# Weight stream operations per inner block of the first feed-forward stage: nine in both halves, or nine and then twelve

## The chip, the cores and the metric

The kernel runs on one core of a Trainium2 chip. The time that counts is the device time of one execution, in microseconds (us). Every number below comes from the times of the kernel before or from one profiled execution of it. TensorE is called PE here, VectorE DVE, ScalarE ACT, GpSimd POOL and SyncE SP.

## The reference

Three stages follow one another: a pooled attention, a feed-forward stage with ELU (here MoE 1), and a feed-forward stage with RMS norm and SwiGLU (MoE 2).

```python
q_pool = q.reshape(B, H, S // 2, 2, D).mean(axis=3)
attn = softmax(q_pool @ k.T / sqrt(D));  x = attn @ v         # x: 1152 tokens x 512
h = x @ w_in                                                  # MoE 1: 512 -> 2048
g = where(h > 0, h, exp(min(h, 0)) - 1);  x = g @ w_out       # 2048 -> 512
xn = x / sqrt(mean(x * x) + 1e-6) * rms_g                     # MoE 2
out = (silu(xn @ w_gate) * (xn @ w_val)) @ w_out2             # 512 -> 1536 -> 512
```

The weights of MoE 1 and MoE 2 arrive as 64-bit floating point numbers; activations are float32.

## The kernel before, in words

Every product is made of three: each operand is split into a high part and a low part, and `product` (lines 162 to 169) adds high x high (L167), low x high (L168) and high x low (L169) for four slices of the inner dimension, so one product of a 128 x 128 x 4 weight tile with a chunk of 384 tokens is twelve matmuls. The 1152 tokens are three chunks, c = 0, 1, 2.

MoE 1 runs in two halves, `hf` = 0 and 1. A half first has eight *inner blocks* (i = 0 to 7): block i multiplies one weight tile with the three chunks, each into a PSUM bank of its own (eight banks go round), and hands each result to `elu`. I write (i, c) for such a unit. `elu` runs, for a unit: on ACT two activations (L183, L184) into a tile e; then it flushes what the unit before left pending, the rounding of its e to the high part `gh` (ACT, L188) and the low part `gl` = e - gh (POOL, L63; for c = 1 of the second half DVE, L69); then steps of the weight stream; then on DVE L187, which reads e and the PSUM bank and so frees the bank; then two more steps of the stream. After the eight blocks comes the *out phase* of the half: products of `gh` and `gl` with the tiles of w_out; for each output tile m first those of blocks 0 to 3 (q = 0) for the three chunks, then those of blocks 4 to 7 (q = 1), slice by slice.

In the second half's out phase the results are added to x (DVE, L607) and squared for the norm (ACT L561; sums on POOL, the last on DVE, L563). The last two output tiles go chunk by chunk, and between them stand the two small PE jobs of the norm of the chunk before: `sums` (six matmuls, L568, which need the DVE's L563), and one product later `scale` (three transposes, L578, which need DVE's reciprocal L572, which needs ACT's root L571). DVE's L581 then scales x.

The *weight stream* turns a 64-bit weight tile into a high and a low float32 part. It is a generator over 68 tiles, nine steps for a tile: ACT L113, DVE L115, (two steps on the tile before, once its buffer is chosen: ACT L141 makes its high part `wh`, POOL L63 its low part `wl`), DVE L120, L122, L124 (after which SP starts a later tile's DMA, L90) and L128. `ws.step(i, k)` runs k steps, and stops early where the stream has got eight tiles ahead of tile i. Nothing is scheduled at run time: each engine runs its instructions in the order in which the program emitted them, so the numbers of steps at the calls set the order on DVE, ACT, POOL and SP.

Of the kernel before, what the change touches and what calls it, by code (L numbers as in the profile page):

```python
# [38 lines left out]
def tile_kernel(ctx: ExitStack, tc: tile.TileContext, qd, kd, vd, w1d, w2d, wgd, wvd, wod, rgd, outd):  # L39
# [120 lines left out]
    cs = lambda c: slice(c * CH, (c + 1) * CH)  # L160

    def product(out, w, a, first, last, ks=range(4)):

        wh, wl = w
        for k in ks:
            ah, al = a(k)
            PE.matmul(out, lhsT=wh[:, k, :], rhs=ah, start=first and k == 0, stop=False)  # L167
            PE.matmul(out, lhsT=wh[:, k, :], rhs=al, start=False, stop=False)  # L168
            PE.matmul(out, lhsT=wl[:, k, :], rhs=ah, start=False, stop=last and k == 3)  # L169

    def xchunk(c):
        return lambda k: (xh[:, k, cs(c)], xl[:, k, cs(c)])
# [3 lines left out]
    def flush():  # L176
        while pending:
            pending.pop(0)()

    def elu(ps, gh, gl, lo):  # L180

        e = hp.tile([128, CH], F32, tag="e", name="e", bufs=4)
        T.activation(out=e, in_=ps, func=AF.Relu, scale=-1.0)  # L183
        T.activation(out=e, in_=e, func=AF.Exp, scale=-1.0)  # L184
        flush()
        ws.step(wi, 1)
        V.scalar_tensor_tensor(out=e, in0=e, scalar=-1.0, in1=ps, op0=ALU.add, op1=ALU.max)  # L187
        pending.append(lambda: (T.copy(gh, e), lo(gl, e, gh)))  # L188
        ws.step(wi, 2)
# [178 lines left out]
    def emit_x(p, xs, a=0, b=QS):  # L368
# [7 lines left out]
        else:  # L376
# [5 lines left out]
    wi = 0  # L382
    ge = tuple(gep.tile([128, NE, CH], F32R, name=f"ge{n}", tag=f"ge{n}") for n in "hl")
    ws = Stream(w_in[:NE] + [w for hf in range(2) for w in
                             (w_in[8:16] if hf else w_in[NE:8]) + [w_out[4 * (2 * hf + q) + m] for m in range(4) for q in range(2)]]
                + [w[i] for i in range(12) for w in (wgd, wvd)] + [wod[i] for i in range(12)])
# [20 lines left out]
    for n in range(ns):  # L407
        p, k = n // NPT, n % NPT
# [112 lines left out]
    for n in range(NE):  # L521
        elu(fb[:, n, 0:CH], ge[0][:, n, :], ge[1][:, n, :], lo_pool)
# [12 lines left out]
    def bank():  # L535

        nonlocal nbank
        n, nbank = nbank % 8, nbank + 1
        if n == 5 and len(psb) == 1:
            with tc.using_default_side("right"):  # L540
                psb.append(ctx.enter_context(tc.tile_pool(name="psC", bufs=3, space=PSUM)))
        return psb[n >= 5].tile([128, 512], F32, tag="b", name="b", bufs=3 if n >= 5 else 5)[:, 0:CH]

    gh, gl = (gp.tile([128, 8, NT], F32R, name=f"g{n}", tag=f"g{n}") for n in "hl")

    def g_quad(hf, q, c):
        return lambda k: ((ge[0][:, k], ge[1][:, k]) if hf == c == q == 0 and k < NE else
                          (gh[:, 4 * q + k, cs(c)], gl[:, 4 * q + k, cs(c)]))
# [40 lines left out]
    wi = 0  # L589
    for hf in range(2):  # L590
        for i in range(8):
            w = ws.get(wi)
            for c in range(3):
                if hf == 0 and c == 0 and i < NE:
                    continue
                ps = bank()
                product(ps, w, xchunk(c), True, True)
                elu(ps, gh[:, i, cs(c)], gl[:, i, cs(c)], lo_dve if c == 1 and hf else lo_pool)
            wi += 1
        flush()  # L600

        def out1(c, m, q, b, w):
            product(b, w, g_quad(hf, q, c), q == 0, q == 1)
            if q == 1:
                x = x2[:, m, cs(c)]
                if hf:
                    V.tensor_tensor(out=x, in0=b, in1=x, op=ALU.add)  # L607
                    norms[c].square(m)
                else:
                    T.copy(x, b)  # L610

        for m in range(2 if hf else 4):
            bs = [bank() for c in range(3)]
            for q in range(2):
                for c in range(3):
                    out1(c, m, q, bs[c], ws.get(wi + q))
                    ws.step(wi + q, 4)
            wi += 2
        if hf:
            T.activation(out=dummy, in_=eps, func=AF.Sqrt)  # L620
            for c in range(3):
                for n in range(4):
                    m, q = 2 + n // 2, n % 2
                    if q == 0:
                        b = bank()
                    out1(c, m, q, b, ws.get(wi + n))
                    if c < 2 or n < 2:
                        ws.step(wi + (n if c == 2 else 0), 3)
                    if c and n == 1:
                        norms[c - 1].sums()  # L630
                    if c and n == 2:
                        norms[c - 1].scale()
            wi += 4
# [103 lines left out]
```

## Time and profile before

| | |
|---|---|
| median of three runs | 696.57 us (695.61 to 697.49) |
| the profiled execution | 696.5 us, span 694.7 us |
| PE busy | 680.0 us (98%) |
| DVE busy | 538.2 us (77%) |
| ACT busy | 415.0 us (60%) |
| POOL busy | 372.6 us (54%) |

The profile's times count from the span's start. The second half of MoE 1 has its inner blocks on PE from 355.8 to 405.5 us, and its out phase from there to about 463 us. A timeline row gives the start, the duration, the engine, the line, the operation, output and inputs, and in brackets how long the engine had been idle and on whom it waited. PE's matmuls overlap: a row of 0.34 us starts 0.17 us after the one before, and the spacing is the cost.

### The profile page before, as it was taken

The page shows a single profiled execution, that of the slowest core. Times are in us where ns is not written, and L with a number is a line of the kernel's source. Part 1 is how long each engine was busy: PE and PEld are TensorE (multiplying, and loading weights), DVE is VectorE, ACT ScalarE, POOL GpSimd, SP SyncE. Part 2 cuts the span into 40 slices and gives each one's busy share as a digit, 9 for nine tenths or more (in the row PEclk, how much of TensorE's full clock was granted, in tenths as well). Part 3 has the DMA queues.
Part 4 walks back from the last instruction along what each step waited for, and adds up shares of the span by engine and source line. Part 5 has one row for each costly group of instructions (what it writes and reads, how often), then busy time and mean ns, then how long its engine had stood idle before and what let it go on. Part 6 is the DMA issues. An engine that isn't in the chain of part 4 may idle for free.

```text
span 694.7 us, 11366 instructions
## 1 busy us (share of the span) xinstructions
PE 680.0 (98%) x4243; PEld 668.1 (96%) x4243; DVE 538.2 (77%) x891; ACT 415.0 (60%) x855; POOL 372.6 (54%) x332
## 2 busy tenths in 40 slices
PE   7999999999999999999999999799999999999998
PEld 6999999989898999999999999799999999999997
DVE  6888889898999877999959999866999876584000
ACT  5888889789888857774447764334444443342000
POOL 5988788897978405674434544532554343342000
PEclk9999999999999999999999999999999999999999
DMA  5423323432432000213422123201323222232000
GB/s 181 144 86 113 128 87 103 144 119 87 134 129 72 1 31 32 92 60 129 145 92 85 67 86 127 91 1 38 116 92 121 92 97 92 87 106 80 35 35 34
DMA packets 21607, 62.34 MB, mean 90 GB/s; under 512 B 2736, under 2 KB 4784, under 8 KB 21552
## 3 DMA queue, kind: packets, MB, share of 16 engines
q1 hardware_dynamic: 21552, 61.62, 26.2%
q8 instruction: 33, 0.54, 0.3%
q14 instruction: 22, 0.18, 0.1%
HBM read 59.25 MB, written 2.36 MB: 89 GB/s over the span
## 4 chain that ended last, share of the span: by engine, by line
PE 78%; DVE 15%; ACT 4%; issue 1%; DVEq 0%; ACTq 0%
PE b L167 16%; PE b L169 16%; PE b L168 16%; PE s L279 10%; PE o L323 9%; PE t L297 8%; DVE p L283 3%; DVE ptl L69 2%; DVE wt L124 2%; DVE wt L128 2%; DVE wt L120 1%; DVE gl L69 1%; DVE e L187 1%; DVE wt L122 1%; ACT gh L188 1%
## 5 line engine op out<-in xcount | busy, mean ns | idle before, releaser
L167 PE MATMUL b<-xh,wh 128*128 128x384 f32 x468 | 157.3, 336 | 0.6 <-ACT sl L638 0.6
L169 PE MATMUL b<-xh,wl 128*128 128x384 f32 x468 | 157.1, 336 | 0.0
L168 PE MATMUL b<-xl,wh 128*128 128x384 f32 x468 | 157.0, 335 | 0.0
L63 POOL TENSOR_TENSOR wl<-wt,wh 128x512 fp32r<-128x512 f32 x68 | 98.4, 1447 | 76.6 <-ACT wh L141 48.2
L283 DVE TENSOR_SCALAR_CACHE_REDUCE p<-s 128x1152 f32<-128x1152 f32 x72 | 97.4, 1354 | 21.1 <-PE s L279 20.7
L69 DVE TENSOR_TENSOR ptl<-t,pth 128x384 fp32r<-128x384 f32 x216 | 106.7, 549 | 3.5 <-ACT pth L305 3.0
L279 PE MATMUL s<-kd,qt 128*128 128x384 f32 x480 | 98.0, 341 | 5.6 <-DVE p L283 4.6
L305 ACT CAST pth<-t 128x384 fp32r<-128x384 f32 x216 | 89.3, 486 | 23.1 <-PE t L297 22.5
L288 ACT ACTIVATE p<-p,st 128x1152 f32<-128x1152 f32 x72 | 91.4, 1269 | 5.2 <-DVE p L283 4.9
L279 PEld LDWEIGHTS s<-kd,qt 128*128 128x128 f32 x480 | 81.5, 188 | 9.0 <-DVE p L283 4.0
L167 PEld LDWEIGHTS b<-xh,wh 128*128 128x128 f32 x468 | 87.9, 188 | 0.9 <-ACT sl L638 0.9
L168 PEld LDWEIGHTS b<-xl,wh 128*128 128x128 f32 x468 | 87.9, 188 | 0.0
L169 PEld LDWEIGHTS b<-xh,wl 128*128 128x128 f32 x468 | 87.9, 188 | 0.0
L297 PE MATMUL t<-ident,p 128*128 128x128 f32 x648 | 85.9, 275 | 0.0
L323 PE MATMUL o<-pth,vd 128*128 128x256 f32 (+1 forms) x288 | 84.4, 315 | 0.0
L297 PEld LDWEIGHTS t<-ident,p 128*128 128x128 f32 x648 | 73.9, 141 | 6.8 <-DVE ptl L69 4.3
L323 PE MATMUL o<-ptl,vd 128*128 128x256 f32 (+1 forms) x288 | 78.4, 295 | 0.0
L113 ACT ACTIVATE wt<-wr 128x512 f32<-128x512 f32 x68 | 45.7, 672 | 51.2 <-POOL wl L63 31.8
L124 DVE SCALAR_TENSOR_TENSOR wt<-wr,wt 128x512 uint32<-128x512 uint32 x68 | 73.2, 1076 | 1.4
L128 DVE CUSTOM_DVE_ANT_0 wt<-wt,we 128x1024 uint16<-128x1024 uint16 x68 | 66.7, 981 | 1.9
L63 POOL TENSOR_TENSOR gl<-e,gh 128x384 fp32r<-128x384 f32 x37 | 40.2, 1087 | 44.5 <-ACT gh L188 42.8
L167 PE MATMUL b<-gh,wh 128*128 128x384 f32 x180 | 61.5, 342 | 0.0
(113 smaller groups left out, 1321.3 us busy)
## 6 DMA issues: line engine op xcount, KB each, us to landing
wr<-in_w_dram SPq DMA_DIRECT2D x32, 512.0 KB, 3.2
rawk<-in_k_dram SPq DMA_DIRECT2D x32, 288.0 KB, 2.9
rawq<-in_q_dram SPq DMA_DIRECT2D x15, 576.0 KB, 3.9
wr<-in_wg_dram SPq DMA_DIRECT2D x12, 512.0 KB, 3.2
wr<-in_wv_dram SPq DMA_DIRECT2D x12, 512.0 KB, 3.2
wr<-in_wo_dram SPq DMA_DIRECT2D x12, 512.0 KB, 3.2
rawv<-in_v_dram SPq DMA_DIRECT2D x16, 288.0 KB, 2.8
out_dram<-o SPq DMA_DIRECT2D x12, 192.0 KB, 1.8
```

What stands on the lines that cost most here:

```text
L63: G.tensor_tensor(out=o, in0=i, in1=f(h), op=ALU.subtract)
L69: V.tensor_tensor(out=o, in0=i, in1=f(h), op=ALU.subtract)
L124: V.scalar_tensor_tensor(out=t, in0=hi, scalar=0x80000000, in1=t, op0=ALU.bitwise_and, op1=ALU.bitwise_xor)
L167: PE.matmul(out, lhsT=wh[:, k, :], rhs=ah, start=first and k == 0, stop=False)
L168: PE.matmul(out, lhsT=wh[:, k, :], rhs=al, start=False, stop=False)
L169: PE.matmul(out, lhsT=wl[:, k, :], rhs=ah, start=False, stop=last and k == 3)
L279: PE.matmul(s[:, m, 0:384], lhsT=a, rhs=b[:, 384 * m:384 * m + 384], start=n == 0, stop=n == len(parts) - 1)
L283: V.tensor_scalar(out=pt, in0=s[:, :, 0:384], scalar1=-0.0625, scalar2=None, op0=ALU.mult, op1=ALU.min, accum_out=st[p][:, 0, TILES[i][4], :])
L288: T.activation(out=pt, in_=pt, func=AF.Exp, scale=-1.0, bias=st[p][:, 0, TILES[i][4], :], accum_out=st[p][:, 1, TILES[i][4], :])
L297: PE.transpose(ps[:, k, :], src[:, 128 * b:128 * b + 128], ident)
L305: T.copy(oh, re(ps))
L323: PE.matmul(self.o[:, 0:self.N], lhsT=v[:, b, :], rhs=(pth, ptl)[u][:, g["buf"], b, g["c0"]:320], start=self.n == 0, stop=self.n == 17)
```

## The change

`elu` takes the number of steps that it runs before L187 as an argument, 1 if nothing is said. The inner blocks of MoE 1 pass 1 in the first half and 2 in the second. With the two steps behind L187 that makes 3 x 3 = 9 steps in a block of the first half and 3 x 4 = 12 in one of the second. The calls for the three units at the end of the attention are as they were.

```diff
-    def elu(ps, gh, gl, lo):
+    def elu(ps, gh, gl, lo, k=1):
...
-        ws.step(wi, 1)
+        ws.step(wi, k)
...
-                elu(ps, gh[:, i, cs(c)], gl[:, i, cs(c)], lo_dve if c == 1 and hf else lo_pool)
+                elu(ps, gh[:, i, cs(c)], gl[:, i, cs(c)], lo_dve if c == 1 and hf else lo_pool, 1 + hf)
```

PE's and SP's instructions stand in the same order in both kernels. On DVE in the second half's inner blocks, from L187 of unit (0, 2), one block before has these nine rows:

```order
L187 SCALAR_TENSOR_TENSOR e<-e,b 128x384
L124 SCALAR_TENSOR_TENSOR wt<-wr,wt 128x512
L128 ISA wt<-wt,we 128x1024
L187 SCALAR_TENSOR_TENSOR e<-e,b 128x384
L115 TENSOR_SCALAR we<-wr 128x512
L187 SCALAR_TENSOR_TENSOR e<-e,b 128x384
L120 TENSOR_SCALAR wt<-wt 128x512
L69 TENSOR_TENSOR gl<-e,gh 128x384
L122 TENSOR_SCALAR wt<-wt 128x512
```

With the change the rows from the same L187 on are (wr, wt and we are the stream's tiles, b the PSUM bank):

```order
L187 SCALAR_TENSOR_TENSOR e<-e,b 128x384
L115 TENSOR_SCALAR we<-wr 128x512
L187 SCALAR_TENSOR_TENSOR e<-e,b 128x384
L120 TENSOR_SCALAR wt<-wt 128x512
L122 TENSOR_SCALAR wt<-wt 128x512
L124 SCALAR_TENSOR_TENSOR wt<-wr,wt 128x512
L128 ISA wt<-wt,we 128x1024
L187 SCALAR_TENSOR_TENSOR e<-e,b 128x384
L115 TENSOR_SCALAR we<-wr 128x512
L69 TENSOR_TENSOR gl<-e,gh 128x384
L187 SCALAR_TENSOR_TENSOR e<-e,b 128x384
L120 TENSOR_SCALAR wt<-wt 128x512
```

Three blocks now hold four tiles' worth of stream rows, and the pattern repeats every three blocks (32 rows) instead of every block (nine). From the first L187 of the half to the last, 13 stream rows more stand on DVE. They are missing later: between that last L187 and the first L572 of the norm DVE has 13 rows fewer. The end of that stretch, on DVE (sq and x are the norm's sums and the stage's result, rr its root):

```order
 L607 TENSOR_TENSOR x_3525<-b,x_3525 128x384
 L563 TENSOR_TENSOR sq<-sq,sqm 128x384
-L120 TENSOR_SCALAR wt<-wt 128x512
-L122 TENSOR_SCALAR wt<-wt 128x512
-L124 SCALAR_TENSOR_TENSOR wt<-wr,wt 128x512
-L128 ISA wt<-wt,we 128x1024
-L607 TENSOR_TENSOR x_3525<-b,x_3525 128x384
-L115 TENSOR_SCALAR we<-wr 128x512
+L607 TENSOR_TENSOR x_3525<-b,x_3525 128x384
 L572 RECIPROCAL rr<-rr 128x3
 L581 SCALAR_TENSOR_TENSOR x_3525<-x_3525,rg,b 128x384 x2
```

No stream row is left between L563 and L572; from L572 on the two kernels are alike on DVE.

## Rows read from the trace of the kernel before

**Rows 1.** Who waited for whom on PE, over the whole span: us in total, times, longest.
```profile
PE b L578 <- DVE rr L572: 2.1, 1, 2.1
PE b L568 <- DVE sq L563: 1.6, 1, 1.6
```

**Rows 2.** The timeline of PE around the norm.
```profile
443.13 0.34 PE L169 MATMUL b<-gh,wl 128*128 128x384 f32 x1
445.10 0.83 PE L568 MATMUL b<-ones,sq 128*128 128x1 f32 x6 [1.64 <-DVE sq L563]
...
450.24 0.54 PE L578 MATMUL b<-ident,rr 128*128 128x128 f32 x3 [2.11 <-DVE rr L572]
450.53 0.42 PE L167 MATMUL b<-gh,wh 128*128 128x384 f32 x1
...
458.45 0.72 PE L568 MATMUL b<-ones,sq 128*128 128x1 f32 x6
...
469.88 0.72 PE L568 MATMUL b<-ones,sq 128*128 128x1 f32 x6
```

**Rows 3.** Busy time by stretch (us from:to, its length; PE, PEld, DVE, ACT and POOL busy, with instructions in brackets; PE's granted clock as a share of 2.4 GHz; share of the DMA engines; GB/s).
```profile
365.00:405.00 40.00, 40.00 (x233) 40.00 (x232) 36.65 (x53) 30.96 (x66) 20.22 (x18) 1.00 0.23 80
...
450.00:451.00 1.00, 0.76 (x6) 0.77 (x7) 0.36 (x2) 0.00 (x0) 0.41 (x1) 1.00 0.08 29
...
452.00:453.00 1.00, 1.00 (x5) 1.00 (x4) 0.47 (x1) 0.50 (x1) 0.94 (x1) 0.50 0.00 0
...
455.00:456.00 1.00, 1.00 (x7) 1.00 (x6) 0.90 (x2) 0.07 (x1) 0.63 (x1) 1.00 0.00 0
```

**Rows 4.** The timeline of DVE at the norm of the first chunk, and its L563 for the second.
```profile
444.49 0.56 DVE L563 TENSOR_TENSOR sq<-sq,sqm 128x384 f32<-128x384 f32 x1 [0.66 <-ACT sqm L561]
444.96 0.42 DVE L120 TENSOR_SCALAR wt<-wt 128x512 f32<-128x512 f32 x1
...
447.56 0.69 DVE L128 CUSTOM_DVE_ANT_0 wt<-wt,we 128x1024 uint16<-128x1024 uint16 x1
...
448.17 0.55 DVE L607 TENSOR_TENSOR x<-b,x 128x384 f32<-128x384 f32 x1
...
450.00 0.18 DVE L572 RECIPROCAL rr<-rr 128x3 f32<-128x3 f32 x1 [0.95 <-ACT rr L571]
...
457.18 0.56 DVE L563 TENSOR_TENSOR sq<-sq,sqm 128x384 f32<-128x384 f32 x1 [0.66 <-ACT sqm L561]
```

**Rows 5.** The timeline of one period of an inner block (from L187 of unit (5, 2) to that of (6, 2)) on DVE, POOL and ACT.
```profile
399.32 0.54 DVE L187 SCALAR_TENSOR_TENSOR e<-e,b 128x384 f32<-128x384 f32 x1
399.79 0.68 DVE L124 SCALAR_TENSOR_TENSOR wt<-wr,wt 128x512 uint32<-128x512 uint32 x1
...
400.49 1.03 POOL L63 TENSOR_TENSOR gl<-e,gh 128x384 fp32r<-128x384 f32 x1 [1.84 <-ACT gh L188]
400.50 1.57 DVE L128 CUSTOM_DVE_ANT_0 wt<-wt,we 128x1024 uint16<-128x1024 uint16 x1
...
401.99 0.54 DVE L187 SCALAR_TENSOR_TENSOR e<-e,b 128x384 f32<-128x384 f32 x1
402.45 0.42 DVE L115 TENSOR_SCALAR we<-wr 128x512 f32<-128x512 uint32 x1
...
402.79 0.54 DVE L187 SCALAR_TENSOR_TENSOR e<-e,b 128x384 f32<-128x384 f32 x1
...
403.16 1.01 POOL L63 TENSOR_TENSOR gl<-e,gh 128x384 fp32r<-128x384 f32 x1 [1.64 <-ACT gh L188]
403.25 1.21 DVE L120 TENSOR_SCALAR wt<-wt 128x512 f32<-128x512 f32 x1
...
404.13 1.48 POOL L63 TENSOR_TENSOR wl<-wt,wh 128x512 fp32r<-128x512 f32 x1
404.45 0.50 ACT L188 CAST gh<-e 128x384 fp32r<-128x384 f32 x1
...
404.98 1.04 DVE L69 TENSOR_TENSOR gl<-e,gh 128x384 fp32r<-128x384 f32 x1 [0.52 <-ACT gh L188]
...
405.94 0.42 DVE L122 TENSOR_SCALAR wt<-wt 128x512 uint32<-128x512 uint32 x1
406.28 0.54 DVE L187 SCALAR_TENSOR_TENSOR e<-e,b 128x384 f32<-128x384 f32 x1
```

**Rows 6.** The timeline of DVE at the start of the backlog: the low part of unit (0, 1).
```profile
363.49 0.83 DVE L69 TENSOR_TENSOR gl<-e,gh 128x384 fp32r<-128x384 f32 x1 [0.73 <-ACT gh L188]
```

**Rows 7.** The timeline of all engines where the last inner block hands over to the out phase: the low parts of block 7 (POOL for c = 0 and c = 2, DVE for c = 1), the last L187, and the three matmuls that read those low parts (L168 of the last slice of q = 1, for c = 0, 1 and 2).
```profile
410.10 1.02 POOL L63 TENSOR_TENSOR gl<-e,gh 128x384 fp32r<-128x384 f32 x1 [1.64 <-ACT gh L188]
...
411.92 1.05 DVE L69 TENSOR_TENSOR gl<-e,gh 128x384 fp32r<-128x384 f32 x1 [0.52 <-ACT gh L188]
...
413.23 0.54 DVE L187 SCALAR_TENSOR_TENSOR e<-e,b 128x384 f32<-128x384 f32 x1
...
413.63 0.34 PE L168 MATMUL b<-gl,wh 128*128 128x384 f32 x1
...
414.39 1.01 POOL L63 TENSOR_TENSOR gl<-e,gh 128x384 fp32r<-128x384 f32 x1 [1.84 <-ACT gh L188]
...
415.75 0.34 PE L168 MATMUL b<-gl,wh 128*128 128x384 f32 x1
...
417.87 0.34 PE L168 MATMUL b<-gl,wh 128*128 128x384 f32 x1
```

## The prediction, on record before the changed kernel was run

> **What bounds the kernel now.** I read the list of waits by PE first, then PE's timeline wherever it lists something, then DVE, ACT and POOL there. PE is busy for 98% of the span, so time is won or lost only where PE stands still or runs at the lower clock. In the stages that the change touches, the list shows two waits, both at the norm of the first chunk: the sums wait 1.6 us for L563 and the transposes 2.1 us for L572, both DVE's [rows 1]. The timeline shows what they cost with what follows. After the last matmul before them (443.13 + 0.17 = 443.30) the sums start at 445.10; the transposes start at 450.24, and the next sums at 458.45 [rows 2]. From those to the third sums (469.88) PE does one product more in 11.43 us without a wait; less 12 x 0.173 = 2.08 us that stretch would be 9.35 us, but 443.30 to 458.45 is 15.15. So 5.8 us are lost here: 1.8 and 2.3 of standing still, and 1.7 because the granted clock falls to 0.50 (the 1.2 GHz level) after the second wait and is back at 1.00 by 455 [rows 3]. These 5.8 us are all that the change can win.
>
> Why is DVE late there? Between L563 (444.49) and L607 (448.17) stand four stream rows; ACT's root, and with it L572, wait behind that L607 [rows 4]. The order shows that the change leaves no stream row there. But DVE is not free before either: in 365 to 405 it is busy for 36.65 of 40.00 us [rows 3]. There a period of DVE takes 406.28 - 399.32 = 6.96 us [rows 5], and PE needs 36 matmuls x 0.173 = 6.2 us for a block. So DVE already falls behind PE by 0.7 us per block, and the question is what four tiles in three blocks instead of three do to that.
>
> **What the change moves.** Nothing is added over the whole program. 13 stream rows (2.6 tiles' worth) go from the out phase into the inner blocks, with their ACT and POOL instructions and their DMAs. I take the DVE queue through three blocks by its new order, with durations from one period before [rows 5].
>
> Unslowed, from start to next start: L187 0.46, L115 0.34, L120 0.45 (0.42 in [rows 4]), L122 0.40, L124 0.71, L128 0.65 (0.69 in [rows 4]), gl on DVE about 0.5 (an estimate: 1.04 less what it waits for POOL). A tile is 2.55. Before, a block is 3 x 0.46 + 0.5 + 2.55 = 4.4. The other 2.5 us are visible: L128 met POOL's gl and ended 0.55 after it (0.9 us late), L120 met the next gl and ended 0.29 after it (0.8), gl met POOL's wl and ended 0.41 after it (0.5), and before that DVE idled 0.52 us for gh. 4.4 + 2.2 + 0.5 = 7.1 against 6.96, so the method holds for the kernel before. L187, which reads PSUM, is never stretched.
>
> Three blocks after: 9 x 0.46 + 3 x 0.5 + 4 x 2.55 = 15.8. POOL has six gl of 1.02 and four wl of 1.48, 12.0 us, where it had 10.6. Placing each POOL instruction right behind its ACT rounding (0.5 us behind L187 for gl), I find nine meetings, in order: L120 behind gl (0, 2) 0.8; L122 behind the wl that follows 1.0; L124 behind gl (1, 0) 0.5; L120 behind a wl 1.0; L122 behind gl (1, 2) 0.5; gl (2, 1) behind a wl 0.3; L128 behind gl (2, 2) 0.9; L122 behind gl (3, 0) 0.8; L124 behind a wl 1.0. That is 6.9 us (before, three blocks have 6.5). Idle for ACT: gl (1, 1) stands two rows behind its L187 and waits 0.35 for gh, gl (2, 1) stands straight behind it and waits 1.3, L187 (3, 1) waits 0.5: 2.2 us (before 1.6). The sum is 24.9 us for three blocks, 8.3 for one; PE needs 18.7.
>
> The first tile begins a little earlier (L115 now stands ahead of the first L187), but L122 and L124 then meet POOL's first gl and wl, and gl (0, 1), at 363.49 before [rows 6], comes out at 364.5. Two periods of 24.9 bring gl (6, 1) to 414.3; the rows from there to the last L187 (three L187, seven stream rows, gl (7, 1), with the first three meetings and the first idle time) take 8.5 us, so it starts at 422.8, against 413.23 [rows 7]. DVE is 9.6 us later at the end of the inner blocks.
>
> **What PE makes of it.** The low parts of block 7 are read at 413.63, 415.75 and 417.87, and were ready at 411.12, 412.97 and 415.40 [rows 7]: a slack of 2.5 to 2.8 us. After: from gl (6, 1) at 414.3 DVE needs 1.7 us to the end of L187 (6, 2) and ACT 0.6 for its gh; then POOL runs gl (6, 2), a wl and gl (7, 0), 3.5 us, to 420.0. gl (7, 1) stands right ahead of the last L187 and ends at 422.9; gl (7, 2) follows that L187 by 0.5, 0.6 and 1.0 us, to 425.0. So PE stands 6.4 us at c = 0, 0.8 more at c = 1 and hardly more at c = 2: 7.2 us. The eight PSUM banks cover the lag up to there: the last inner product starts near 403.3 and needs the L187 eight units earlier, (5, 0), which this puts at 402.0.
>
> After such a standstill I take the clock to fall as it did after 2.1 us at the norm, for the same price, 1.7 us; the trace has no longer wait in dense matmuls, so the bounds are 0 and twice that.
>
> At the norm PE is then about 9 us later, and DVE, with eight rows fewer up to L563, is not: both waits of the first chunk go, with their low clock, 5.8 us. What is late next is L563 of the second chunk: it ends at 457.74, 7.5 us behind the transposes at 450.24 [rows 2, 4], a chain through L581, ACT and L607. At full clock PE gets from those transposes to the next sums in 0.3 + 36 x 0.173 = 6.5 us, so 0.9 us of wait appears there (bounds 0 and 1.5).
>
> DMA: a transfer starts behind each L124, now every 6.2 us instead of 7, on DMA engines at a share of 0.23 [rows 3]; I cost it at nothing. ACT gets a third of a tile's two rows more per block and has room: it is busy for 31 of 40 us [rows 3].
>
> Sum against the profiled execution: 696.5 - 5.8 + 7.2 + 1.7 + 0.9 = 700.5 us. The median of the runs, 696.57, is the same for this purpose.
>
> The page "SBUF — State Buffer" of the Trainium skill, section "SBUF: two separate sides", says that VectorE and GpSimd take a shared port pair as an exclusive lock for a whole instruction. The meetings in [rows 5] agree (a DVE row ends 0.3 to 0.55 us after the POOL row it met); read to the full, with all 12.0 us of POOL taken from DVE, a period would be 30 us and the time about 712, but before only 2.2 of a block's 3.5 us were taken, so I give that reading 2%.
>
> **The rivals.**
> *DVE catches up (faster).* If the ACT waits vanish under the longer queue, a period is 15.8 + 6.9 = 22.7, 2.2 less; over 2.3 periods that is 5.1 us, PE stands 2.1 us, the clock holds: 696.5 - 5.8 + 2.1 + 0.9 = 693.7. For it: DVE has a backlog, so most inputs should lie ready. Against: before, with a backlog too, gl waits 0.52 for gh in every block, since L188 comes straight behind an L187 in the same queue. It decides at a period of about 23.3 us. 13%.
> *About even.* Half of that idle time goes, or the clock holds: PE stands 4.7 us, 696.5 - 5.8 + 4.7 + 0.9 = 696.3, with a low clock 698.0. 21%.
> *The banks run out too.* One more meeting of 0.9 us per three blocks puts the last L187 2 us later and (5, 0) past 403.3; PE then stands inside the blocks as well and the clock falls twice: 696.5 - 5.8 + 9.2 + 3.4 + 0.9 = 704.2. 8%, with the reading above.
> *The change does nothing*, because the limit of eight tiles ahead stops the added steps. The order speaks against it: 13 rows have moved, and the limit binds only in the last unit. 2%, at 696.5.
>
> **Numbers.** The forecast, 700.5, has the other 56%; its own range, with a stand of 6 to 8 us and a clock price of 0.7 to 2.7, is 698.3 to 702.3. About 0.3%, 2.1 us, is what a measurement of this kernel can tell from no change: faster means under 694.5, slower over 698.7. Faster is the first rival, 0.13; the same the second and the last, 0.23; slower the rest, 0.64. The range for eight in ten reaches from the upper edge of the first rival to the bank rival: 694.6 to 703.8.
>
> **What would show it.** Right: on PE's list of waits, L578 and L568 of the first chunk are gone, and a wait for gh or gl of about 6 us stands at c = 0 of q = 1, near 414; the last L187 at about 423; a granted clock of 0.5 behind it; a wait of some 0.9 us at the second sums. Wrong: three blocks on DVE in less than 23.3 us, or the last L187 before 418. If DVE takes 24.9 and the time still falls, PE's slack was misread.

## The result and the profile after

The changed kernel takes 700.45 us (median of 6 runs, 698.74 to 701.68), the kernel before 696.86 (6 runs beside it). The ratio is 1.0053, with a 95% interval of 1.0036 to 1.0070: slower by 3.6 us, where 700.5 was forecast. One of the eleven executions of experiment 6 below took 1356.01 us and is left out of its ratio.

The profiled execution of the changed kernel took 701.68 us, its span 699.9. One thing has to be set right before rows are compared. The second half's first inner matmul starts at 356.74 there and at 355.57 before (the 355.8 given with the profile before is 0.2 late), although the instructions up to it are the same. In the run of experiment 2 below, whose edit lies only in the last out phase, it starts at 356.38; so this start moves from run to run, and 1.17 us is taken off the later times of after wherever they are set against before.

Who waited for whom on PE, of the kernel after (us in total, times, longest), where [rows 1] had the two waits at the norm:
```profile
PE b L167 <- ACT gh L188: 4.2, 1, 4.2
...
PE b L168 <- POOL gl L63: 1.3, 1, 1.3
...
PE b L568 <- DVE sq L563: 0.8, 1, 0.8
```
L578 is gone from the list and L568 has one wait instead of one of 1.6 at the first sums. In their place stand a wait for gh and one for gl, one time each. PE's timeline, which answers to [rows 2], puts places to them:
```profile
356.74 0.34 PE L167 MATMUL b<-xh,wh 128*128 128x384 f32 x1
...
453.21 0.72 PE L568 MATMUL b<-ones,sq 128*128 128x1 f32 x6
...
455.97 0.49 PE L578 MATMUL b<-ident,rr 128*128 128x128 f32 x3
...
463.48 0.83 PE L568 MATMUL b<-ones,sq 128*128 128x1 f32 x6 [0.75 <-DVE sq L563]
...
468.81 0.34 PE L167 MATMUL b<-xh,wh 128*128 128x384 f32 x1
```
The first sums and the transposes carry no bracket any more: the norm of the first chunk is free of waits. Only the second sums wait, 0.75 us by the bracket (0.92 from the last matmul before them, the measure of the prediction). The two large waits are at the hand-over from the last inner block to the out phase. The timeline of all engines there answers to [rows 7]:
```profile
417.11 0.99 POOL L63 TENSOR_TENSOR gl<-e,gh 128x384 fp32r<-128x384 f32 x1 [2.71 <-ACT gh L188]
...
418.06 1.46 POOL L63 TENSOR_TENSOR wl<-wt,wh 128x512 fp32r<-128x512 f32 x1
...
418.40 0.49 ACT L188 CAST gh<-e 128x384 fp32r<-128x384 f32 x1
...
418.95 0.44 PE L167 MATMUL b<-gh,wh 128*128 128x384 f32 x1 [4.18 <-ACT gh L188]
...
419.49 1.18 POOL L63 TENSOR_TENSOR gl<-e,gh 128x384 fp32r<-128x384 f32 x1
...
420.71 0.69 PE L168 MATMUL b<-gl,wh 128*128 128x384 f32 x1 [1.32 <-POOL gl L63]
...
423.46 0.55 DVE L187 SCALAR_TENSOR_TENSOR e<-e,b 128x384 f32<-128x384 f32 x1
```
On POOL stand, one behind the other, gl of unit (6, 2), a tile's wl and gl of (7, 0). PE waits first for the rounding of unit (7, 0) on ACT, then for that gl. The wait is for DVE all the same: ACT's rounding of the unit before, (6, 2), waits until 416.52 for its L187 at 415.95, the rounding of (7, 0) comes behind it in ACT's queue, and the last L187 starts at 423.46, 9.1 us later than the 413.23 of [rows 7] once the 1.17 is taken off. The matmul at 420.71 also shows the clock: it takes 0.69, where those of [rows 7] take 0.34. The 0.44 of the one at 418.95 does not, for the granted clock is still 1.00 from 418 to 419. The windows (columns as in [rows 3]) say the same:
```profile
365.00:405.00 40.00, 40.00 (x233) 40.00 (x232) 36.69 (x53) 28.51 (x58) 19.56 (x18) 1.00 0.27 91
...
386.84:411.51 24.67, 24.67 (x144) 24.67 (x143) 22.42 (x32) 17.19 (x36) 11.99 (x10) 1.00 0.25 86
...
416.00:418.00 2.00, 0.00 (x0) 0.00 (x0) 2.00 (x5) 1.50 (x5) 0.89 (x1) 1.00 0.71 258
...
420.00:421.00 1.00, 0.28 (x1) 0.29 (x2) 1.00 (x1) 0.97 (x3) 0.66 (x1) 0.50 0.00 0
426.00:427.00 1.00, 1.00 (x5) 1.00 (x5) 0.97 (x2) 0.00 (x0) 1.00 (x1) 0.61 0.00 0
```
From 416 to 418 PE does nothing while DVE is busy for the whole stretch; at 420 the granted clock is 0.50 (1.2 GHz), and it is still low in the row from 426 to 427, whose 0.61 is a mean of both levels. Up to 405 PE has no gap; the row from 386.84 is one of three blocks, to which the steps below come back. From 365 to 405 DVE shows the same busy share as before (36.69 us, against 36.65 in [rows 3]), so the share alone tells nothing of the lag that builds up.

The difference, in three stretches of PE:

| stretch of PE | before | after | difference |
|---|---|---|---|
| first inner matmul to the late L168 (355.57 to 413.63; 356.74 to 420.71) | 58.06 | 63.97 | +5.9 |
| from there to the first sums (before without their wait, to 443.30) | 29.67 | 32.50 | +2.8 |
| from there to the first matmul of MoE 2 (463.64; 468.81) | 20.34 | 15.60 | -4.7 |
| sum | 108.07 | 112.07 | +4.0 |

The first row is standing still, the second the low clock, the third the waits and the low clock that the norm no longer has, less the new wait at the second sums. The 463.64 of before is PE's first matmul of MoE 2:
```profile
463.64 0.34 PE L167 MATMUL b<-xh,wh 128*128 128x384 f32 x1
```

### The profile page after: what moved, and what is told of

Same layout as the page of the kernel before. It is cut to its first block, busy times and chain, and to the rows that moved or that the text cites. A ratio compares the mean times of both kernels' runs of the same rounds, so it can differ in the third digit from the quotient of the medians.

```text
span 699.9 us, 11357 instructions
## 1 busy us (share of the span) xinstructions
PE 681.2 (97%) x4243; PEld 669.4 (96%) x4243; DVE 539.7 (77%) x891; ACT 415.0 (59%) x855; POOL 372.7 (53%) x332
## 4 chain that ended last, share of the span: by engine, by line
PE 86%; DVE 9%; ACT 2%; issue 1%; DMA 1%; SPq 0%; POOL 0%; ACTq 0%; DVEq 0%; POOLq 0%
PE b L167 19%; PE b L168 19%; PE b L169 18%; PE s L279 10%; PE o L323 9%; PE t L297 8%; DVE p L283 2%; DVE ptl L69 2%; DVE wt L124 1%; DVE wt L122 1%; DMA rawk<-in_k_dram 1%; DVE wt L120 1%; ACT xh L583 1%; DVE wt L128 1%; DVE e L187 0%
## 5 line engine op out<-in xcount | busy, mean ns | idle before, releaser
L168 PE MATMUL b<-xl,wh 128*128 128x384 f32 x468 | 157.0, 335 | 0.0
L69 DVE TENSOR_TENSOR ptl<-t,pth 128x384 fp32r<-128x384 f32 x216 | 106.6, 547 | 3.7 <-ACT pth L305 3.1
L168 PEld LDWEIGHTS b<-xl,wh 128*128 128x128 f32 x468 | 87.9, 188 | 0.0
L124 DVE SCALAR_TENSOR_TENSOR wt<-wr,wt 128x512 uint32<-128x512 uint32 x68 | 77.8, 1144 | 1.5
L128 DVE CUSTOM_DVE_ANT_0 wt<-wt,we 128x1024 uint16<-128x1024 uint16 x68 | 62.5, 919 | 1.7
```

Source lines behind the costliest of these rows:

```text
L69: V.tensor_tensor(out=o, in0=i, in1=f(h), op=ALU.subtract)
L124: V.scalar_tensor_tensor(out=t, in0=hi, scalar=0x80000000, in1=t, op0=ALU.bitwise_and, op1=ALU.bitwise_xor)
```

## The experiments

The theory (A): DVE is behind PE throughout the inner blocks of the second half; rows that the change adds there lengthen its queue, and the whole lag falls on PE where the out phase reads block 7. The rows in themselves cost nothing where DVE has idle time. The rival (B): what counts is that the operations come earlier at all, or how many they are (pressure on buffers, DMA or POOL), wherever they are put.

**Experiment 1: the same 24 operations in the out phase of the first half.**
```
-                    ws.step(wi + q, 4)
+                    ws.step(wi + q, 4 if hf else 5)
```


> Nine steps per inner block everywhere, as before; the 24 steps are added to the first half's out phase instead (five per product instead of four). DVE idles for about 7 us between 339 and 361 there, so the 9.5 us that 2.6 tiles take should make it late by about 2 us at the start of the second half, and later blocks run at 7 us as before. Theory A (DVE's queue in the second half's inner blocks is what delays PE): the last L187 near 415, no or almost no stand of PE at c = 0 of q = 1, both waits at the first norm gone, 0.8 us of wait at the second sums: 696.9 - 5.8 + 0.8 = 691.9, range 690.5 to 693.5. Theory B (the stream costs time by being further ahead: weight buffers or transfers in the way): it is as far ahead as in the changed kernel, so the time is near 700.

Measured: 692.21 us (691.61 to 692.65) against 696.75; ratio 0.9931 (0.9918 to 0.9943). The windows of the kernel before and of this one, at the end of the first half's out phase (columns as in [rows 3]):
```profile
352.00:358.00 6.00, 6.00 (x37) 6.00 (x35) 2.24 (x4) 2.27 (x6) 1.34 (x1) 1.00 0.44 165
```
```profile
352.00:358.00 6.00, 6.00 (x36) 6.00 (x35) 5.83 (x8) 2.34 (x4) 2.95 (x2) 1.00 0.44 160
```
DVE was busy for 2.24 of these 6 us and now is for 5.83, with PE without a gap in both. There is no wait at the hand-over, and PE's timeline at the norm shows this:
```profile
443.31 0.72 PE L568 MATMUL b<-ones,sq 128*128 128x1 f32 x6
...
453.58 0.83 PE L568 MATMUL b<-ones,sq 128*128 128x1 f32 x6 [0.76 <-DVE sq L563]
```
The first sums follow the last matmul at once, and the second wait 0.76. Rival B falls: nearly as many stream rows (12 more than before by the last L187, against 13 in the changed kernel), put earlier still, and the kernel is 8.2 us faster than the changed one. It is also 4.5 us faster than the kernel before. Two things did not come as expected: DVE enters the half 5.1 us late and not 2 (its first L187 starts at 364.00, against 358.93), and its blocks then take 6.44 to 6.46 us and not 7, so that the last L187 still starts at 413.99, no earlier than before. The gain is thus not a DVE that leaves the blocks earlier; experiment 5 comes back to it.

**Experiment 2: no operations in the last out phase** beyond its first chunk, and nothing put in their place before.
```
-                    if c < 2 or n < 2:
+                    if c == 0:
```


> The kernel before, without the stream's steps between the products of the second and third chunk in the last out phase (they run later, in MoE 2). Theory A: the first sums still wait 1.8 us (as many rows stand ahead of L563), the transposes' wait of 2.3 us and the low clock, 1.7 us, go, the second sums wait 0.9 us: 696.9 - 4.0 + 0.9 = 693.8, range 692.5 to 695. Rival: the rows left out are missed in MoE 2 and PE waits there for weights: 696 or more, with a wait of PE on wl or wh after 480.

Measured: 694.75 us against 696.75; ratio 0.9972 (0.9962 to 0.9982). The transposes wait no more and the clock stays up; the first sums still wait 1.62 us, the second 0.76:
```profile
PE b L568 <- DVE sq L563: 2.4, 2, 1.6
```
PE's list has no wait for weights, so the rows left out are not missed in MoE 2. Between the two matmuls of the table above, 105.19 us pass where before had 108.07, so 2.9 less; the medians differ by 2.0. So the operations given out at the norm are the cause of one of the two waits there. The other, at the first sums, is not theirs: a tile's rows from before them still stand ahead of L563, up to 443.74, because DVE comes out of the inner blocks as late as before (the last L187 at 414.00).

**Experiments 3 and 4: twelve operations in the first four blocks alone, and in the last four alone.**
```
-    elu(..., 1 + hf)
+    elu(..., 1 + (hf and i < 4))
```
```
-    elu(..., 1 + hf)
+    elu(..., 1 + (hf and i >= 4))
```


> Twelve steps in blocks 0 to 3 of the second half, nine in 4 to 7. Theory A: DVE is 5.3 us late after block 3 and stays so, since its queue does not run dry afterwards: last L187 near 418.5, PE stands 2.8 us, clock price 0 to 3 us, first sums wait 0 to 2 us: 696 to 699. Rival (rows in the last blocks are what delays the hand-over): with nine rows in the last blocks DVE catches up, no stand, 692 to 693.

> Nine steps in blocks 0 to 3 of the second half, twelve in 4 to 7. Theory A: the same as with the early blocks, within 1 us, at the last L187 and in the time: 696 to 699. Rival (rows in the last blocks are what delays the hand-over): as the changed kernel, 700, and at least 2 us slower than with the early blocks.

Measured: 695.57 us for the first (ratio 0.9982, 0.9972 to 0.9991) and 698.41 for the second (1.0022, 1.0011 to 1.0033). The time of the second lies in the range that was written down, that of the first 0.4 us below it; that the two would agree within 1 us was wrong by far. The last L187 starts at 416.11 in the early variant and at 419.31 in the late one, 2.7 and 5.6 us later than before, each counted from the half's first matmul (355.80 and 356.01). At the hand-over the early rows leave a stand of 0.5 us; the late ones leave 2.2 us in three pieces, and a longer wait at the first sums:
```profile
PE b L568 <- DVE sq L563: 2.3, 2, 1.9
...
PE b L167 <- ACT gh L188: 1.3, 1, 1.3
...
PE b L168 <- POOL gl L63: 1.0, 2, 0.6
```
The granted clock of the late variant behind its first sums (columns as in [rows 3]):
```profile
455.00:456.00 1.00, 1.00 (x5) 1.00 (x4) 0.66 (x2) 0.01 (x1) 0.00 (x0) 0.50 0.00 0
```
The clock is at 0.50 from 450 to 456 there; in the early variant it is back at 1.00 from 451. The profiled run of the late variant took 700.52 us, 2.1 above its median, so these are the waits of a long run, and the comparison of the two rests on the medians.

As many rows were added in both, so a count of rows does not tell them apart. The blocks that kept nine operations do: in the early variant they take 6.44 us each on DVE (L187 at 391.15, 397.59, 404.02, 410.46), in the late one 6.94 or 6.95, as good as the 6.96 of [rows 5]. The work in such a block is the same to the row. What differs is where in the block a tile's rows fall, because twelve operations do not go into the pattern of nine evenly. Over four blocks this makes 2 of the 3 us between the two last L187; where the rest comes from the runs do not show. That called for a test by itself.

**Experiment 5: three operations once, ahead of the first block of the second half,** and nine in each block, as before.
```
             w = ws.get(wi)
+            if hf and i == 0:
+                ws.step(wi, 3)
```


> Nine steps per inner block as before, but three steps more ahead of the second half, so that the same nine rows fall into the places that they have in the two runs with a period of 6.44 us (five steps in the first out phase; the last four blocks of the early run) instead of 6.96. If the places alone set the period: 6.4 us per block, the last L187 near 410.6 instead of 413.2, L563 about 2.5 us earlier, no wait at the first sums, about 1 us at the transposes, the clock holds: 692.9, range 692 to 694.5. If the period was shorter in those runs because work had been taken away elsewhere, it stays at 7 us and the time at 696.5.

Measured: 692.82 us (691.91 to 694.54); ratio 0.9949 (0.9937 to 0.9962). This is the timeline of DVE, POOL and ACT in one block, as [rows 5] shows it for the kernel before:
```profile
391.22 0.55 DVE L187 SCALAR_TENSOR_TENSOR e<-e,b 128x384 f32<-128x384 f32 x1
...
391.59 1.01 POOL L63 TENSOR_TENSOR gl<-e,gh 128x384 fp32r<-128x384 f32 x1 [2.83 <-ACT gh L188]
...
391.68 1.21 DVE L120 TENSOR_SCALAR wt<-wt 128x512 f32<-128x512 f32 x1
...
392.56 1.48 POOL L63 TENSOR_TENSOR wl<-wt,wh 128x512 fp32r<-128x512 f32 x1
...
392.92 1.40 DVE L122 TENSOR_SCALAR wt<-wt 128x512 uint32<-128x512 uint32 x1
...
394.25 0.54 DVE L187 SCALAR_TENSOR_TENSOR e<-e,b 128x384 f32<-128x384 f32 x1
...
394.71 1.04 DVE L124 SCALAR_TENSOR_TENSOR wt<-wr,wt 128x512 uint32<-128x512 uint32 x1
...
394.82 0.51 ACT L188 CAST gh<-e 128x384 fp32r<-128x384 f32 x1 [0.38 <-DVE e L187]
...
396.39 0.55 DVE L69 TENSOR_TENSOR gl<-e,gh 128x384 fp32r<-128x384 f32 x1
...
397.66 0.55 DVE L187 SCALAR_TENSOR_TENSOR e<-e,b 128x384 f32<-128x384 f32 x1
```
The same nine rows take 397.66 - 391.22 = 6.44 us. In [rows 5] one stream row stands between the L187 of chunk 1 (402.79) and its gl (L69); ACT's rounding comes 1.66 us behind that L187, at 404.45, so DVE idles 0.52 for it, and gl's 1.04 hold 0.5 of waiting for POOL. Here two stream rows stand between (L124 and L128), ACT rounds 0.57 us behind the L187, at 394.82, and gl has no bracket, takes 0.55 and meets nothing. Three rows still meet POOL (1.21, 1.40 and 1.04, where alone they take 0.42, 0.42 and 0.68). Half a microsecond per block brings the last L187 to 409.75, where it was 413.23. With that the first sums no longer wait; PE's row has no bracket:
```profile
443.47 0.72 PE L568 MATMUL b<-ones,sq 128*128 128x1 f32 x6
```
The four stream rows between L563 and L607, on which the prediction blames the wait for L572, still stand there (441.28 to 443.07): with L563 at 440.80 instead of 444.49 they delay nobody, and the wait of about 1 us that was expected at the transposes did not come. Between the two matmuls of the table 103.30 us pass, as in experiment 1: 4.8 less than before. By the trace three operations are therefore enough for what experiment 1 won with 24; by the medians they win 3.9 us and those 4.5. Experiment 1 too runs its blocks at 6.46, and it has no stream row left between L563 and L572. How much of its gain is the phase and how much the emptier norm, it does not separate; both kernels end with the one wait at the second sums.

**Experiment 6: the changed kernel, with block 7 read later.** The out phase does q = 0 for m = 0 and 1 first, then q = 1 for both.
```
+        if hf:
+            bs = [[bank() for c in range(3)] for m in range(2)]
+            for q in range(2):
+                for m in range(2):
+                    for c in range(3):
+                        out1(c, m, q, bs[m][c], ws.get(wi + 2 * m + q))
+                        ws.step(wi + (0, 1, 1, 3)[2 * q + m], 4)
```


> The changed kernel with the first two output tiles of the second half's out phase in another order: blocks 0 to 3 for both, then blocks 4 to 7 for both, so that PE asks for block 7 some 6.4 us later. Theory A (PE stands because block 7's low parts come late from DVE's queue): DVE's inner blocks stay as in the changed kernel (24.7 us for three), the stand of 5.5 us goes down to a wait of about 1.4 us for a bank, the clock holds, both waits at the first norm stay away: 696.8 - 5.8 + 1.4 + 0.8 = 693.1, range 692 to 695. If the loss of the changed kernel lay elsewhere (weights, transfers, the clock by itself), the time stays at 699 or more.

Measured: 696.94 us against 696.76; ratio 1.0001 (0.9992 to 1.0011). This is 3.5 us faster than the changed kernel, and 3.8 slower than expected. DVE's queue through the blocks is as in the changed kernel (three blocks in 24.67 us, the last L187 at 422.38), yet of the stand of 5.9 us there is left one wait of 1.2 for a bank:
```profile
PE b L568 <- DVE sq L563: 2.3, 2, 1.6
...
PE b L167 <- DVE e L187: 1.2, 1, 1.2
...
PE b L578 <- DVE rr L572: 0.5, 1, 0.5
```
So the lag of DVE costs PE only where its results are read early, as theory A has it. The miss is at the norm, where the waits came back. DVE's timeline there:
```profile
445.96 0.56 DVE L563 TENSOR_TENSOR sq<-sq,sqm 128x384 f32<-128x384 f32 x1 [0.66 <-POOL wl L63]
446.43 0.42 DVE L122 TENSOR_SCALAR wt<-wt 128x512 uint32<-128x512 uint32 x1
446.89 0.69 DVE L124 SCALAR_TENSOR_TENSOR wt<-wr,wt 128x512 uint32<-128x512 uint32 x1
447.61 0.69 DVE L128 CUSTOM_DVE_ANT_0 wt<-wt,we 128x1024 uint16<-128x1024 uint16 x1
448.22 0.42 DVE L115 TENSOR_SCALAR we<-wr 128x512 f32<-128x512 uint32 x1
448.56 0.55 DVE L607 TENSOR_TENSOR x<-b,x 128x384 f32<-128x384 f32 x1
```
Four stream rows stand between L563 and L607, the picture of [rows 4]. The new order holds a tile longer, so the limit of eight tiles ahead stops the stream in between and the operations come late, at the norm again: between the last L187 and L563 DVE runs 21 stream rows where the changed kernel runs 25, and the other four follow L563. The expectation had left the limit out.

**Experiment 7: the changed kernel, with DVE's gl on POOL too.**
```
-    elu(..., lo_dve if c == 1 and hf else lo_pool, 1 + hf)
+    elu(..., lo_pool, 1 + hf)
```


> The changed kernel with the low part of chunk 1 on POOL as in the first half, so that DVE has one row fewer per block and no longer idles for gh, while POOL has 15.1 us of work in three blocks instead of 12. Theory A by the same working: 9 x 0.46 + 4 x 2.55 = 14.3, meetings at the same share of POOL's time 8.7, idle about 0.5: 23.5 us for three blocks instead of 24.7, the last L187 about 3 us earlier, a stand of 2 to 3 us; time 694 to 698. If the rows of the stream alone set the period, it stays at 24.7 and the time at 700.

Measured: 700.68 us against 696.76; ratio 1.0060 (1.0047 to 1.0073), the time of the changed kernel. The stand is the same:
```profile
PE b L167 <- ACT gh L188: 4.3, 1, 4.3
...
PE b L168 <- POOL gl L63: 1.1, 1, 1.1
```
Three blocks of this kernel by the windows, beside which the row from 386.84 of the kernel after is to be held:
```profile
386.59:411.16 24.57, 24.57 (x143) 24.57 (x142) 23.76 (x29) 17.17 (x36) 16.07 (x13) 1.00 0.25 86
```
DVE has three rows fewer (29 for 32), which alone take about 0.5 us each, and is busy for 23.76 us instead of 22.42: POOL has three gl more and is busy for 4.1 us more, and DVE's rows beside them stretch. The idle time goes down (24.57 - 23.76 = 0.8 us, from 2.2), and the meetings take that too. DVE is now busy for 9.5 us more than the 14.3 of its rows alone, where the expectation had 8.7: POOL was busy for 16.07 us and not for 15.1, and of that about as large a share falls on DVE as was expected (59%, against 58%). The idle time is 0.8 where 0.5 was expected. That the stretch comes from POOL is read from DVE's rows that end just behind POOL's, as in [rows 5]; no run takes POOL's work away. The Trainium skill says of this move, in "Perfetto Trace Analysis", section "Optimizing Scalar/DVE Operations", that the two engines share an SBUF port and that shifting work between them might not help; the 0.1 us won of 24.67 agrees.

## Why the prediction was right

Its own steps, with the 1.17 us taken off all times of after.

- **Three blocks on DVE, 24.9 us.** The L187 of units (0, 1), (3, 1) and (6, 1) start 24.66 and 24.67 us apart. (The nine meetings as listed add up to 6.8, not 6.9; with the other terms this gives 24.8.) DVE's timeline, with the three idle times of the list and one of its nine meetings:
```profile
362.18 0.55 DVE L187 SCALAR_TENSOR_TENSOR e<-e,b 128x384 f32<-128x384 f32 x1 [1.10 <-ACT e L184]
...
365.55 0.55 DVE L69 TENSOR_TENSOR gl<-e,gh 128x384 fp32r<-128x384 f32 x1
...
373.73 0.56 DVE L69 TENSOR_TENSOR gl<-e,gh 128x384 fp32r<-128x384 f32 x1 [0.25 <-ACT gh L188]
...
380.91 0.84 DVE L69 TENSOR_TENSOR gl<-e,gh 128x384 fp32r<-128x384 f32 x1 [1.23 <-ACT gh L188]
...
383.65 1.56 DVE L128 CUSTOM_DVE_ANT_0 wt<-wt,we 128x1024 uint16<-128x1024 uint16 x1
...
386.84 0.56 DVE L187 SCALAR_TENSOR_TENSOR e<-e,b 128x384 f32<-128x384 f32 x1 [0.49 <-ACT e L184]
...
411.51 0.55 DVE L187 SCALAR_TENSOR_TENSOR e<-e,b 128x384 f32<-128x384 f32 x1 [0.49 <-ACT e L184]
```
  The idle times are 0.25, 1.23 and 0.49 where 0.35, 1.3 and 0.5 were forecast, at the rows named; L128 behind gl (2, 2) takes 1.56, 0.9 over its own 0.69. The other eight meetings stand at the rows named too, each within about 0.2 us of its forecast. The rival in which the waits for ACT vanish fell with this, and so did the reading by which all of POOL's time is taken from DVE (30 us).
- **Where the lag ends.** gl (0, 1) at 364.4 (forecast 364.5), gl (7, 0) out at 419.5 (420.0), the last L187 at 422.3 (422.8).
- **The stand, 7.2 us.** Measured 5.9, all of it at c = 0, where 6.4 was forecast. The 0.8 at c = 1 did not come, because PE reaches c = 1 and c = 2 at the low clock, and so later than the forecast took it.
- **The clock, 1.7 us.** This term was mis-sized: the second row of the table gives 2.8. The bounds of 0 and twice 1.7 held it. The two errors, 1.3 too much and 1.1 too little, nearly cancel: 8.7 measured for both, 8.9 forecast. The mechanism was right, but that the total came out so close is luck.
- **The norm.** Both waits of the first chunk are gone, as forecast, and the second sums wait 0.92 by the prediction's measure where 0.9 was said (its own 7.5 - 6.5 is 1.0). The third row of the table is -4.7; by the terms it is -5.8 + 0.9 = -4.9.
- **The banks.** PE has no gap in the blocks (40.00 of 40.00 us); that rival fell.

The forecast change was +4.0 in the trace, which measured +4.0, and the medians give 3.6. What the prediction did not see is that the 6.96 us it took from a block of before is no property of the nine rows. It walked the order of after row by row and so was right without knowing it; its statement that DVE falls behind by 0.7 us per block holds for one phase of the pattern only (6.44 against the 6.2 that PE needs in the other).

Left open: why the clock stayed low for longer here than at the norm of before. The length of the stand alone does not decide: in the profiled run of experiment 4 a single wait of 1.94 us at the first sums is followed by 0.50 until 456, about as long as behind the 5.9 us here. No run varies the load on PE behind a stand. Nor does any run shift the phase of the twelve-operation pattern, so whether the 24.7 us could be shorter by another placement of the same rows is not shown.

## What to carry to other kernels

Before work is moved to an earlier place in an in-order queue, look there for the engine's idle time and not only for its busy share: 24 operations cost 3.6 us where DVE already lagged, and the kernel won 4.5 with them where it had 3.8 of 6 us free (not by the idle time alone, it may be: experiment 5 won 3.9 by the phase of the blocks). Where two engines disturb each other, walk one period of the queue row by row with its meetings and waits; the sum of the durations alone would have given 15.8 us for three blocks that took 24.7. And where a repeating pattern runs just slower than its consumer, try shifting its phase: three operations given once won 3.9 us, nearly as much as the 24.

## What was not expected of the hardware

- The same nine rows of DVE, five of the stream, three L187 and one gl, take 6.96 us per block in one phase and 6.44 in another (experiment 5), with nothing changed but which of them stands beside which row of POOL and ACT.
- A row moved from DVE to POOL gave DVE almost nothing back: 24.57 for 24.67 us (experiment 7).
- After the 5.9 us of standing still the granted clock was 0.50 until after 426, and back at 1.00 from 427; at the norm of before it was back by 455 after a wait that ended at 450.24 [rows 2, 3]. And waits of like length at the first sums do not always cost the clock: in the profiled run of experiment 3 it fell to 0.50 after 1.36 us, in that of experiment 6 it stayed at 1.00 after 1.57 and 0.49, and in that of experiment 4 it stayed at 0.50 until 456 after 1.94.
